# Loads in order of use, three weight groups, and a first feed-forward pass shared by two halves

## The chip, the cores and the metric

One core of a Trainium2 chip. The metric is the device time of one execution in microseconds; medians are over all runs of a kernel in one job, ratios over its fast runs alone. "The profile" is the trace of one execution; its clock starts at the span's start. Its engines: PE is TensorE (matmuls; PEld its weight loads), DVE VectorE, ACT ScalarE, POOL GpSimd, SP SyncE, which here only issues transfers.

## The reference, cut to what matters

Windowed attention with a few global keys, then a gated feed-forward block on its output. B = 4 batches, H = 8 heads, S = 768 positions, D = 64; the feed-forward goes 512 to 1536 to 512.

```python
scores = q @ k.T / sqrt(D) + bias          # per head
scores = where(is_global | is_local, scores, -1e9)   # 8 global keys, window of 96
a = softmax(scores)
x = (a @ v) as [B*S, H*D]                  # 3072 x 512
out = (maximum(x @ w_gate, 0) * (x @ w_val)) @ w_out
```

The kernel cuts the work into eight "halves" (a batch has two, of 384 positions). Each half needs its attention, then its feed-forward.

## The kernel before: the parts that the change touches

The loads, the one POOL queue that issues v and the weights, and the casts of q and k from fp32 to bf16 (for half 0: q on DVE, k on POOL):

```python
load_qk(0, 0, 2)                 # SP queue, heads 0 and 1 of half 0
...
nc.vector.memset(vbuf[0]...)     # ones, the whole buffer
load_qk(0, 2, 4)
load_v_globals(0); spread_v_globals(0)
load_v(0, 0) ... load_v(0, 3)    # POOL queue, casts fp32 to bf16
load_qk(0, 4, 8)
load_w(wgA, ...); load_w(wvA, ...)       # first 512 columns
load_half(1)                             # q, k and v of half 1
load_w(wgB, ...); load_w(wvB, ...)       # the other 1024 columns
load_w(wo_sb, ...)
...
eng = nc.vector if s == 0 and i == 0 else nc.gpsimd     # in piece_cast
```

The order of work: half 0's attention alone; then stages, in each of which one half's feed-forward pieces are woven with the next half's attention pieces. The schedule is fixed by hand, so each engine runs its instructions in this order:

```python
for i, (_, f) in enumerate(attention_pieces(0)):
    f()
    ...                          # masks of the later heads between pieces
nc.vector.memset(vbuf[1]...)     # fill of the second v buffer, here
...
for c in range(NHALF):
    if c + 2 < NHALF:
        load_half(c + 2)         # q and k on SP, three or five v loads on POOL
    a_items = attention_pieces(c + 1) if c + 1 < NHALF else []
    f_items = ffn_pieces(c)      # 24 gate/value pieces (4 matmuls each), 6 output pieces (6 each)
    ...                          # spread a_items over 0.9 of f_items
```

The softmax here doesn't subtract the row's maximum and nothing guards it: scores larger than these inputs give would overflow.

## Time and profile before

| | |
|---|---|
| median of 3 runs | 307.01 us (305.67 to 307.62) |
| profiled span | 302.9 us |
| PE busy | 247.9 us |
| PE idle up to 53 us | 37 us |
| one later stage | 31.7 us, about 2 us of it idle |

A row of the timeline reads: start, duration, engine, line, operation, tile written and tiles read, shape, count, and in brackets how long the engine had idled before and what ended that. L249 or L245 is the transpose of a head pair's q and k, the first step of its attention; "xT" is its last step. Between them lie kT (k transposed and put in its place), es (the exponentials of the scores, multiplied by the masks) and AV (es times v). I use three markers throughout: the *second transpose* of half 0, the end of the *last xT* of a half, and the *first transpose of half 3*.

### The profile page before, as it was taken

The numbers are of one execution on the slowest core, as the hardware profiler recorded it, in microseconds if no ns is written. First come the engines' busy times: TensorE is split into PE (matmuls) and PEld (weight loads), VectorE is DVE, ScalarE is ACT, GpSimd is POOL, SyncE is SP. The second block draws the span as 40 slices with busy tenths as digits, with TensorE's granted clock in tenths as the row PEclk, the third lists the DMA queues.
The fourth block names the chain that finished last, engine by engine and source line by source line (L and its number), as shares of the span: only waits on it lengthen the run. The fifth ranks groups of instructions, "written<-read, shape, count | busy, mean of one in ns | idle before, by whom it ended". The sixth has DMA issues, their size and how long they took to land.

```text
span 302.9 us, 4741 instructions
## 1 busy us (share of the span) xinstructions
PE 247.9 (82%) x1665; PEld 148.0 (49%) x1680; DVE 169.1 (56%) x477; ACT 168.3 (56%) x361; POOL 60.9 (20%) x105
## 2 busy tenths in 40 slices
PE   0025351998899889989898989988998899899995
PEld 0014230665466545655565546654664466545652
DVE  7624554567358644765466637773567457653420
ACT  1109640375737664767565765666575738664321
POOL 4940006913103400340226000400031000000000
PEclk9999999999999999999999999999999999999999
DMA  3999999905192614432760518001700110001002
GB/s 105 156 235 251 230 223 193 94 2 37 69 209 69 39 37 146 145 25 46 110 203 6 43 63 257 0 2 71 233 13 0 69 37 1 0 37 71 2 0 104
DMA packets 51208, 27.50 MB, mean 91 GB/s; under 512 B 27952, under 2 KB 46896, under 8 KB 51184
## 3 DMA queue, kind: packets, MB, share of 16 engines
q0 software_dynamic: 30800, 7.91, 25.5%
q1 hardware_dynamic: 20384, 19.30, 21.3%
q8 instruction: 13, 0.21, 0.3%
q14 instruction: 11, 0.09, 0.1%
HBM read 28.38 MB, written 6.29 MB: 114 GB/s over the span
## 4 chain that ended last, share of the span: by engine, by line
PE 69%; DVE 12%; ACT 10%; POOL 3%; DMA 3%; issue 3%; ACTq 0%; POOLq 0%
PE ff_ps L372 20%; PE ff_ps L363 18%; PE ff_ps L353 17%; DVE xT L331 6%; PE av_ps L314 5%; PE qk_ps L286 5%; PE tp L245 3%; DMA vbuf<-in_v_dram 3%; ACT lnd L323 2%; ACT grelu L356 2%; ACT rcp L328 2%; POOL vbuf L135 2%; DVE ht L365 1%; DVE qp L251 1%; DVE vbuf L399 1%
## 5 line engine op out<-in xcount | busy, mean ns | idle before, releaser
L372 PE MATMUL ff_ps<-wo_sb,ht 128*128 128x512 bf16 x273 | 67.2, 379 | 0.8
L365 DVE TENSOR_TENSOR ht<-ff_ps,grelu 128x384 bf16<-128x384 f32 x96 | 53.1, 554 | 24.3 <-PE ff_ps L363 21.6
L331 DVE TENSOR_TENSOR xT<-av_ps,rcp 64x384 bf16<-64x384 f32 x64 | 35.5, 555 | 46.2 <-ACT rcp L328 33.5
L356 ACT ACTIVATE grelu<-ff_ps 128x384 bf16<-128x384 f32 x96 | 47.3, 493 | 24.3 <-DVE ht L365 13.8
L353 PE MATMUL ff_ps<-xT,wgB 128*128 128x384 bf16 x256 | 52.0, 325 | 4.8 <-DVE ht L365 4.8
L363 PE MATMUL ff_ps<-xT,wvB 128*128 128x384 bf16 x256 | 52.0, 325 | 3.5 <-ACT grelu L356 3.5
L289 ACT ACTIVATE es<-qk_ps 128x432 bf16<-128x432 f32 (+2 forms) x96 | 49.1, 538 | 4.0 <-PE qk_ps L286 3.2
L298 DVE TENSOR_TENSOR es<-es,m_all 128x432 bf16<-128x432 bf16 (+6 forms) x144 | 40.6, 314 | 18.1 <-ACT es L289 17.0
L372 PEld LDWEIGHTS <-ht 128*128 128x128 bf16 x288 | 27.2, 97 | 26.9
L286 PE MATMUL qk_ps<-qp,kT 128*128 128x432 bf16 (+6 forms) x144 | 33.6, 303 | 7.9 <-ACT es L289 7.9
L245 PE MATMUL tp<-ident,qk 128*128 128x128 bf16 x192 | 17.8, 233 | 26.0 <-DVE qk L234 12.8
L323 ACT ACTIVATE lnd<-av_ps 64x384 f32<-64x384 f32 x64 | 31.0, 485 | 12.8 <-PE av_ps L314 11.1
L314 PE MATMUL av_ps<-es,vbuf 128*128 128x216 bf16 (+5 forms) x288 | 28.9, 236 | 7.2 <-DVE xT L331 6.6
L234 POOL CAST qk<-qs 128x384 bf16<-128x384 f32 x28 | 14.3, 510 | 101.0 <-DMA qs<-in_q_dram 35.0
L353 PEld LDWEIGHTS <-wgB 128*128 128x128 bf16 x256 | 23.8, 97 | 19.5 <-issue 6.4
L314 PEld LDWEIGHTS <-vbuf 128*128 128x128 bf16 x288 | 23.9, 102 | 17.3 <-issue 8.2
L363 PEld LDWEIGHTS <-wvB 128*128 128x128 bf16 x256 | 23.7, 97 | 17.4 <-issue 4.7
L135 POOL DMA_DIRECT2D vbuf<-in_v_dram x28 | 24.8, 894 | 22.4 <-PE av_ps L314 22.4
L245 PEld LDWEIGHTS <-qk 128*128 128x128 bf16 x192 | 14.0, 104 | 31.0 <-DVE qk L234 12.8
L353 PE MATMUL ff_ps<-xT,wgA 128*128 128x384 bf16 x128 | 28.0, 343 | 1.3 <-DVE xT L331 1.3
L363 PE MATMUL ff_ps<-xT,wvA 128*128 128x384 bf16 x128 | 27.4, 339 | 0.0
L377 ACT COPY osb<-ff_ps 128x512 f32<-128x512 f32 x24 | 14.0, 585 | 23.2 <-PE ff_ps L372 22.9
(54 smaller groups left out, 153.5 us busy)
## 6 DMA issues: line engine op xcount, KB each, us to landing
out_dram<-osb SPq DMA_DIRECT2D x24, 256.0 KB, 2.0
qs<-in_q_dram SPq DMA_DIRECT2D x7, 768.0 KB, 5.5
ks<-in_k_dram SPq DMA_DIRECT2D x7, 768.0 KB, 7.9
vbuf<-in_v_dram POOLq DMA_DIRECT2D x24, 120.0 KB, 4.0
wo_sb<-in_moe_w_out_dram POOLq DMA_DIRECT2D x1, 1536.0 KB, 35.6
wgB<-in_moe_w_gate_dram POOLq DMA_DIRECT2D x1, 1024.0 KB, 25.4
wvB<-in_moe_w_val_dram POOLq DMA_DIRECT2D x1, 1024.0 KB, 29.5
wgA<-in_moe_w_gate_dram POOLq DMA_DIRECT2D x1, 512.0 KB, 11.3
```

Of the source, the lines that this page charges most:

```text
L245: nc.tensor.matmul(tp[:, i, n * 128 : (n + 1) * 128], lhsT=qk[:, i, n], rhs=ident, is_transpose=True, start=(i == 0 and n == 0), stop=(i = ...
L286: nc.tensor.matmul(ps[:, c : c + n_], lhsT=kt[:, j, :], rhs=qd[:, :, :, a : a + w], start=True, stop=True)
L289: nc.scalar.activation(es[:, 0:cols], ps[:, 0:cols], AF.Exp, bias=0.0, scale=scale)
L298: nc.vector.tensor_mul(e4, e4, mk)
L314: nc.tensor.matmul(av3[:, :, a : a + w], lhsT=vb[:, j, z0 : z0 + 128], rhs=es[:, c : c + NN * w].rearrange("k (n p) -> k n p", n=NN), star ...
L323: nc.scalar.activation(ln[o0 : o0 + 64], av[d0 : d0 + 64, 0:QH], AF.Ln, bias=0.0, scale=1.0)
L331: nc.vector.tensor_tensor(xT_of[s][r, p, :], av_of[s, p, e_][r, 0:QH], rc[r], op=ALU.mult)
L353: nc.tensor.matmul(psg[:, 0:QH], lhsT=wg_of(dc, fc), rhs=xT[:, dc, :], start=(dc == 0), stop=(dc == N_DC - 1))
L356: nc.scalar.activation(gr, psg[:, 0:QH], AF.Relu, bias=0.0, scale=1.0)
L363: nc.tensor.matmul(psv[:, 0:QH], lhsT=wv_of(dc, fc), rhs=xT[:, dc, :], start=(dc == 0), stop=(dc == N_DC - 1))
L365: nc.vector.tensor_tensor(ht[:, fc, :], psv[:, 0:QH], st["gr"], op=ALU.mult)
L372: nc.tensor.matmul(ps2, lhsT=ht[:, fc, n * 128 : (n + 1) * 128], rhs=wo_sb[:, fc, :], start=(fc == 0), stop=(fc == N_FC - 1))
```

## The change

The intent: order the loads by when they are used, cut gate and value weights into three column groups of 512, and let feed-forward work start while weights still come in. Halves 0 and 1 therefore share the first pass over the weights: groups 0 and 1 are used by half 0, then by half 1, and only then group 2 by both. The mask arithmetic partly moves from DVE to POOL, sixteen mask Exps become eight larger ones ahead of the attention, and most fills move to POOL.

```diff
-    load_qk(0, 0, 2)
...
+    for p in range(HP):
+        load_qk(0, 2 * p, 2 * p + 2)          # all of half 0 first
...
+    spread_v_globals(0)
+    load_w_group(0)
...
+    load_w_group(1)
+    load_v_half(1)
+    load_w_group(2)
     load_w(wo_sb, moe_w_out, 0, DM)
...
-            eng = nc.vector if s == 0 and i == 0 else nc.gpsimd
+            eng = nc.vector if s == 0 and (i == 0 or p == 0) else nc.gpsimd
...
+    def load_qk_after(s):                     # a 1-element DVE memset holds the load back
+        qs_of[s] = stage.tile(...); ks_of[s] = stage.tile(...)
+        for t in (qs_of[s], ks_of[s]):
+            nc.vector.memset(t[0:1, 0, 0:1], 0.0)
+        load_qk(s, 0, H)
...
+    for _, f in attention_pieces(0):
+        f()
+    load_qk_after(1)
+    f1_0, f2_0 = ffn_pieces(0)                # f1: 24 gate/value pieces, f2: 6 output pieces
+    G2 = 2 * GW                               # 8 pieces: one column group
+    weave(f1_0[0:G2], [])
+    a1 = attention_pieces(1)
+    weave(f1_0[G2 : 2 * G2], a1, 0.4, 1.4)    # what does not fit follows bare
+    rest_of_start()                           # fills for the second batch, on POOL
+    f1_1, f2_1 = ffn_pieces(1)
+    weave(f1_1[0 : 2 * G2], [])
+    load_qk_after(2)
+    load_v_half(2)
+    weave(f1_0[2 * G2 :], [])
+    load_qk_after(3)
+    load_v_half(3)
+    weave(f1_1[2 * G2 :] + f2_0 + f2_1, attention_pieces(2))
+
+    for c in range(2, NHALF):                 # stages as before
...
```

More of the change, by code (lines that the diff above doesn't have):

```diff
@@ L84 @@
     ident = const.tile([128, 128], BF16)
-    nc.vector.memset(ident, 0.0)
     vbuf = [const.tile([128, NT, (2 * H + 1) * D], BF16, name=f"vbuf{i}") for i in range(2)]
@@ L88, with w_of @@
     qp = [const.tile([128, 2, QH], BF16, name=f"qp{i}") for i in range(4)]
-    GA = 4
-    wgA = const.tile([128, N_DC, GA * 128], BF16)
-    wvA = const.tile([128, N_DC, GA * 128], BF16)
-    wgB = const.tile([128, N_DC, DFF - GA * 128], BF16)
-    wvB = const.tile([128, N_DC, DFF - GA * 128], BF16)
+    GW = 4
+    wg = [const.tile([128, N_DC, GW * 128], BF16, name=f"wg{i}") for i in range(N_FC // GW)]
+    wv = [const.tile([128, N_DC, GW * 128], BF16, name=f"wv{i}") for i in range(N_FC // GW)]
     wo_sb = const.tile([128, N_FC, DM], BF16)
     m_all = const.tile([128, H, 2, NN, WQ], BF16)
-    def wg_of(dc, fc):
-        t, f = (wgA, fc) if fc < GA else (wgB, fc - GA)
-        return t[:, dc, f * 128 : (f + 1) * 128]
-    def wv_of(dc, fc):
-        t, f = (wvA, fc) if fc < GA else (wvB, fc - GA)
-        return t[:, dc, f * 128 : (f + 1) * 128]
+    def w_of(t, dc, fc):
+        f = fc % GW
+        return t[fc // GW][:, dc, f * 128 : (f + 1) * 128]
     qs_of, ks_of = {}, {}
@@ L137, in load_v, with load_v_half @@
             in_=v[b, :, KT * j : KT * j + n, :].rearrange("h p d -> p h d"))
-    def load_half(s):
+    def load_v_half(s):
         b, half = divmod(s, 2)
-        load_qk(s, 0, H)
         if half == 0:
@@ L144, in load_half @@
             spread_v_globals(b)
-            for j in range(4):
-                load_v(b, j)
-        else:
-            for j in range(4, NT):
-                load_v(b, j)
+        for j in range(4) if half == 0 else range(4, NT):
+            load_v(b, j)
     def load_w(dst, src, f0, f1):
         nc.gpsimd.dma_start(out=dst, in_=src[:, f0:f1].rearrange("(c p) f -> p c f", p=128))
-    def ones_of(i, j0, j1):
-        t = vbuf[i][:, j0:j1, :].rearrange("p j (h z) -> p j h z", z=D)[:, :, 0 : 2 * H + 1 : 2, :]
-        nc.vector.memset(t, 1.0)
@@ L159, with load_w_group, fill @@
-    load_qk(0, 0, 2)
+    def load_w_group(i):
+        load_w(wg[i], moe_w_gate, i * GW * 128, (i + 1) * GW * 128)
+        load_w(wv[i], moe_w_val, i * GW * 128, (i + 1) * GW * 128)
+    def fill(eng, i, j):
+        eng.memset(vbuf[i][:, j, :].bitcast(mybir.dt.uint32), 0x3F803F80)
+    def load_qk_after(s):
+        qs_of[s] = stage.tile([128, H, NN * D], FP32, name="qs")
+        ks_of[s] = stage.tile([128, H, NN * D], FP32, name="ks")
+        for t in (qs_of[s], ks_of[s]):
+            nc.vector.memset(t[0:1, 0, 0:1], 0.0)
+        load_qk(s, 0, H)
@@ L160 @@
+    for p in range(HP):
+        load_qk(0, 2 * p, 2 * p + 2)
+    nc.vector.memset(ident, 0.0)
+    for j in range(3):
+        fill(nc.vector, 0, j)
+    dd = setupp.tile([128, 2, NN, WQ], FP32)
+    pos = setupp.tile([NG, NN, WQ], FP32)
+    relg = setupp.tile([NG, NN, WQ], FP32)
     rel = setupp.tile([128, NN, WQ], FP32)
-    nc.gpsimd.iota(rel, [[1, NN], [NN, WQ]], base=NG, channel_multiplier=-1,
+    sel = setupp.tile([128, NN, WQ], FP32)
+    steps = [[1, NN], [NN, WQ]]
+    nc.gpsimd.iota(pos, steps, base=0, channel_multiplier=0,
@@ L162 @@
                    allow_small_or_imprecise_dtypes=True)
+    nc.gpsimd.iota(relg, steps, base=0, channel_multiplier=-1,
+                   allow_small_or_imprecise_dtypes=True)
+    nc.gpsimd.iota(rel, steps, base=NG, channel_multiplier=-1,
+                   allow_small_or_imprecise_dtypes=True)
+    nc.gpsimd.affine_select(out=sel, in_=rel, compare_op=ALU.is_ge, fill=BIG, base=NG,
+                            pattern=steps, channel_multiplier=-1)
+    nc.gpsimd.affine_select(out=dd[:, 1], in_=sel, compare_op=ALU.is_ge, fill=BIG,
+                            base=NL - 1 - NG, pattern=[[-1, NN], [-NN, WQ]],
+                            channel_multiplier=1)
@@ new lines @@
+    ga = setupp.tile([NG, NN, WQ], FP32)
+    gb = setupp.tile([NG, NN, WQ], FP32)
+    gc_ = setupp.tile([NG, NN, WQ], FP32)
+    gd = setupp.tile([NG, NN, WQ], FP32)
+    nc.vector.tensor_scalar(gb, pos, float(KT + NL - 2), BIG, op0=ALU.is_gt, op1=ALU.mult)
+    nc.vector.tensor_scalar(ga, pos, float(NL - 1), BIG, op0=ALU.is_lt, op1=ALU.mult)
+    nc.vector.tensor_add(ga, ga, gb)
+    nc.vector.tensor_scalar(gd, relg, 0.0, BIG, op0=ALU.is_ge, op1=ALU.mult)
+    nc.vector.tensor_scalar(gc_, relg, float(NL - 1), 1.0, op0=ALU.is_le, op1=ALU.mult)
@@ L163 @@
+    nc.vector.tensor_mul(gd, gd, gc_)
+    nc.vector.tensor_add(gd, gd, gb)
+    nc.vector.tensor_copy(dd[:, 0], dd[:, 1])
+    nc.vector.tensor_scalar(dd[0:NG, 1], ga, float(NL), None, op0=ALU.add)
+    nc.vector.tensor_scalar(dd[0:NG, 0], gd, float(NL), None, op0=ALU.add)
     nc.gpsimd.affine_select(out=ident, in_=ident, compare_op=ALU.not_equal,
@@ L165 @@
                             channel_multiplier=1)
-    pos = setupp.tile([NG, NN, WQ], FP32)
-    nc.gpsimd.iota(pos, [[1, NN], [NN, WQ]], base=0, channel_multiplier=0,
-                   allow_small_or_imprecise_dtypes=True)
-    relg = setupp.tile([NG, NN, WQ], FP32)
-    nc.gpsimd.iota(relg, [[1, NN], [NN, WQ]], base=0, channel_multiplier=-1,
-                   allow_small_or_imprecise_dtypes=True)
-    nc.vector.memset(vbuf[0].rearrange("p j z -> p (j z)").bitcast(mybir.dt.uint32), 0x3F803F80)
@@ L173 @@
-    load_qk(0, 2, 4)
-    load_v_globals(0)
-    spread_v_globals(0)
-    load_v(0, 0)
-    load_v(0, 1)
-    load_v(0, 2)
-    load_v(0, 3)
-    load_qk(0, 4, 8)
-    load_w(wgA, moe_w_gate, 0, GA * 128)
-    load_w(wvA, moe_w_val, 0, GA * 128)
-    load_half(1)
-    load_w(wgB, moe_w_gate, GA * 128, DFF)
-    load_w(wvB, moe_w_val, GA * 128, DFF)
-    load_w(wo_sb, moe_w_out, 0, DM)
-    for t in qp:
-        nc.vector.memset(t[64:128, 0, :], 0.0)
-        nc.vector.memset(t[0:64, 1, :], 0.0)
@@ L191 @@
-    for p in range(HP):
-        nc.vector.memset(kT[0][p][:, 3, 32:128], 0.0)
-    dm = setupp.tile([128, NN, WQ], FP32)
-    df = setupp.tile([128, NN, WQ], FP32)
-    pa = setupp.tile([128, NN, WQ], FP32)
-    pb = setupp.tile([128, NN, WQ], FP32)
-    nc.vector.tensor_scalar(pa, rel, 0.0, BIG, op0=ALU.is_lt, op1=ALU.mult)
-    nc.vector.tensor_scalar(pb, rel, float(NL - 1), BIG, op0=ALU.is_gt, op1=ALU.mult)
-    nc.vector.tensor_add(dm, rel, pa)
-    nc.vector.tensor_add(dm, dm, pb)
-    nc.vector.tensor_copy(df, dm)
@@ L204 @@
-    ga = setupp.tile([NG, NN, WQ], FP32)
-    gb = setupp.tile([NG, NN, WQ], FP32)
-    gc_ = setupp.tile([NG, NN, WQ], FP32)
-    nc.vector.tensor_scalar(gb, pos, float(KT + NL - 2), BIG, op0=ALU.is_gt, op1=ALU.mult)
-    nc.vector.tensor_scalar(ga, pos, float(NL - 1), BIG, op0=ALU.is_lt, op1=ALU.mult)
-    nc.vector.tensor_add(ga, ga, gb)
-    nc.vector.tensor_scalar(dm[0:NG], ga, float(NL), None, op0=ALU.add)
-    nc.vector.tensor_scalar(ga, relg, 0.0, BIG, op0=ALU.is_ge, op1=ALU.mult)
-    nc.vector.tensor_scalar(gc_, relg, float(NL - 1), 1.0, op0=ALU.is_le, op1=ALU.mult)
@@ L214 @@
-    nc.vector.tensor_mul(ga, ga, gc_)
-    nc.vector.tensor_add(ga, ga, gb)
-    nc.vector.tensor_scalar(df[0:NG], ga, float(NL), None, op0=ALU.add)
-    def build_masks(h):
-        nc.scalar.activation(m_all[:, h, 0], df, AF.Exp, bias=0.0, scale=-slopes[h])
-        nc.scalar.activation(m_all[:, h, 1], dm, AF.Exp, bias=0.0, scale=-slopes[h])
+    for j in range(3, NT):
+        fill(nc.vector, 0, j)
+    for i, t in enumerate(qp):
+        nc.gpsimd.memset(t[64:128, 0, :].bitcast(mybir.dt.uint32), 0)
+        nc.gpsimd.memset(t[0:64, 1, :].bitcast(mybir.dt.uint32), 0)
+        if i == 0:
+            load_v_globals(0)
+            load_v(0, 0)
+            load_v(0, 1)
+        if i == 1:
+            load_v(0, 2)
+            load_v(0, 3)
@@ L223 @@
+    spread_v_globals(0)
+    load_w_group(0)
+    for p in range(HP):
+        nc.gpsimd.memset(kT[0][p][:, 3, 32:128].bitcast(mybir.dt.uint32), 0)
+        nc.gpsimd.memset(kT[0][p][:, 6, NG + 48 : 128].bitcast(mybir.dt.uint32), 0)
+    load_w_group(1)
+    load_v_half(1)
+    load_w_group(2)
+    load_w(wo_sb, moe_w_out, 0, DM)
+    for h in range(H):
+        nc.scalar.activation(m_all[:, h], dd, AF.Exp, bias=0.0, scale=-slopes[h])
     xT_of = {}
@@ L352, in gate @@
             for dc in range(N_DC):
-                nc.tensor.matmul(psg[:, 0:QH], lhsT=wg_of(dc, fc), rhs=xT[:, dc, :],
+                nc.tensor.matmul(psg[:, 0:QH], lhsT=w_of(wg, dc, fc), rhs=xT[:, dc, :],
                                  start=(dc == 0), stop=(dc == N_DC - 1))
@@ L362, in val @@
             for dc in range(N_DC):
-                nc.tensor.matmul(psv[:, 0:QH], lhsT=wv_of(dc, fc), rhs=xT[:, dc, :],
+                nc.tensor.matmul(psv[:, 0:QH], lhsT=w_of(wv, dc, fc), rhs=xT[:, dc, :],
                                  start=(dc == 0), stop=(dc == N_DC - 1))
@@ L378, in outp, with weave @@
                 nc.sync.dma_start(out=out_v[c, n], in_=osb)
-        items = []
+        f1 = []
         for fc in range(N_FC):
-            items.append((0.65, lambda fc=fc: gate(fc)))
-            items.append((0.65, lambda fc=fc: val(fc)))
+            f1.append((0.65, lambda fc=fc: gate(fc)))
+            f1.append((0.65, lambda fc=fc: val(fc)))
+        f2 = []
         for n in range(NN):
             for part in range(2):
-                items.append((1.3, lambda n=n, part=part: outp(n, part)))
-        return items
-    for h in range(2):
-        build_masks(h)
-    pieces = attention_pieces(0)
-    for i, (_, f) in enumerate(pieces):
-        f()
-        if i in (4, 8, 12):
-            h = {4: 2, 8: 4, 12: 6}[i]
-            build_masks(h)
-            build_masks(h + 1)
-    nc.vector.memset(vbuf[1].rearrange("p j z -> p (j z)").bitcast(mybir.dt.uint32), 0x3F803F80)
-    for p in range(HP):
-        nc.vector.memset(kT[0][p][:, 6, NG + 48 : 128], 0.0)
-        nc.vector.memset(kT[1][p][:, 3, 32:128], 0.0)
-        nc.vector.memset(kT[1][p][:, 6, NG + 48 : 128], 0.0)
-    for c in range(NHALF):
-        if c + 2 < NHALF:
-            load_half(c + 2)
-        a_items = attention_pieces(c + 1) if c + 1 < NHALF else []
-        f_items = ffn_pieces(c)
+                f2.append((1.3, lambda n=n, part=part: outp(n, part)))
+        return f1, f2
+    def weave(f_items, a_items, first=0.0, last=0.9):
         total = sum(t for t, _ in f_items)
@@ L414, with rest_of_start @@
             done += t
-            while ai < len(a_items) and (ai + 0.5) / len(a_items) * 0.9 * total <= done:
+            while (ai < len(a_items)
+                   and (first + (ai + 0.5) / len(a_items) * (last - first)) * total <= done):
                 a_items[ai][1]()
                 ai += 1
-        assert ai == len(a_items)
+        for _, f in a_items[ai:]:
+            f()
+    def rest_of_start():
+        for p in range(HP):
+            nc.gpsimd.memset(kT[1][p][:, 3, 32:128].bitcast(mybir.dt.uint32), 0)
+            nc.gpsimd.memset(kT[1][p][:, 6, NG + 48 : 128].bitcast(mybir.dt.uint32), 0)
+        for j in range(NT):
+            fill(nc.gpsimd, 1, j)
+    for _, f in attention_pieces(0):
+        f()
+    load_qk_after(1)
[14 more added lines that the diff above has]
+    for c in range(2, NHALF):
+        if c + 2 < NHALF:
+            load_qk(c + 2, 0, H)
+            load_v_half(c + 2)
+        f1, f2 = ffn_pieces(c)
+        weave(f1 + f2, attention_pieces(c + 1) if c + 1 < NHALF else [])
 _INS = ['q', 'k', 'v', 'n_global', 'n_local', 'moe_w_gate', 'moe_w_val', 'moe_w_out']
```

## The prediction

> **What bounds the kernel now.** I read the page first, then the table by stretches, then the chain in order of time, then the timeline of the first 70 us.
>
> ```profile
> span 302.9 us, 4741 instructions
> PE 247.9 (82%) x1665; PEld 148.0 (49%) x1680; DVE 169.1 (56%) x477; ACT 168.3 (56%) x361; POOL 60.9 (20%) x105
> ```
>
> PE is busy 248 of 303 us. The table by stretches (PE, PEld, DVE, ACT, POOL busy; granted clock; DMA share; GB/s) says where the other 55 us are.
>
> ```profile
> 10.00:19.00 9.00, 0.70 (x6) 0.44 (x7) 2.77 (x9) 1.20 (x4) 7.45 (x10) 1.00 1.37 205
> 19.00:30.00 11.00, 6.03 (x39) 4.08 (x38) 5.86 (x22) 7.62 (x22) 1.14 (x3) 1.00 1.32 245
> 30.00:41.40 11.40, 5.13 (x32) 3.38 (x30) 6.56 (x18) 7.57 (x17) 0.00 (x0) 1.00 1.14 230
> 41.40:53.00 11.60, 4.18 (x16) 1.59 (x13) 5.49 (x16) 2.05 (x5) 4.80 (x7) 1.00 1.33 202
> 53.00:85.00 32.00, 30.04 (x205) 17.98 (x208) 19.32 (x55) 19.04 (x41) 13.39 (x23) 1.00 0.54 51
> 85.00:117.00 32.00, 29.79 (x205) 17.85 (x206) 18.90 (x52) 20.21 (x44) 6.25 (x11) 1.00 0.46 89
> ```
>
> Up to 53 us PE works 16 us and idles 37; after that each 32 us stretch idles about 2. So only the first 53 us hold anything to win. From there a stage (one half's feed-forward woven with the next half's attention) lasts 31.7 us, the step between its first matmuls in the chain:
>
> ```profile
> 84.81 0.65 PE ff_ps L353 x4
> ...
> 116.52 0.65 PE ff_ps L353 x4
> ```
>
> The timeline splits the 37 us:
>
> ```profile
> 17.21 1.02 POOL L152 DMA_DIRECT2D wo_sb<-in_moe_w_out_dram  x1 [0.85 <-DMA vbuf<-in_v_dram]
> 18.23 0.96 POOL L234 CAST qk<-ks 128x384 bf16<-128x384 f32 x2
> 18.80 0.50 PE L245 MATMUL tp<-ident,qk 128*128 128x128 bf16 x3 [5.49 <-POOL qk L234]
> ...
> 20.88 0.80 PE L245 MATMUL tp<-ident,qk 128*128 128x128 bf16 x6 [1.58 <-DVE kT L264]
> ...
> 23.99 1.50 ACT L289 ACTIVATE es<-qk_ps 128x432 bf16<-128x432 f32 x3
> ...
> 42.67 1.14 DVE L331 TENSOR_TENSOR xT<-av_ps,rcp 64x384 bf16<-64x384 f32 x2 [1.85 <-ACT rcp L328]
> ...
> 44.67 3.23 DVE L399 MEMSET vbuf<- 128x3808 uint32 x1 [0.86 <-issue]
> ...
> 48.20 0.62 POOL L124 DMA_DIRECT2D vbuf<-in_v_dram  x1 [27.15 <-DVE vbuf L399]
> ...
> 52.99 0.94 PE L245 MATMUL tp<-ident,qk 128*128 128x128 bf16 x6 [6.09 <-POOL qk L234]
> ```
>
> To 18.8 us: the first k cast stands behind the weight issues on POOL, the last of which waits for a v load. From 18.8 to 43.8: attention of half 0 alone, 25.0 us of a chain through PE, ACT and DVE, PE half idle. From 46.9 to 53.0: POOL waits for the fill of the second v buffer, issues five v loads, and only then casts half 1, while PE waits 6.1 us. That last gap is an order of instructions, not missing weights.
>
> **What the Trainium skill says.** DMA: Bandwidth & Descriptors, "Issuing engines are not separate DMA queues": transfers started by different engines share the same 16 DMA engines. The trace agrees: between 24 and 30 us the two queues move nearly equal packet counts (571 and 571 in 24 to 26), each well below its rate alone. TensorE: Matmul & The Clock Gate, "What's actually happening": PE runs at half clock until it has been busy for about 3.4 us, and falls back after an idle window. The trace agrees: four 384-column matmuls take 1.28 us at 53.7 and 0.65 us from 56.2 on, 3.2 us after PE resumed. The same page, "Architectural detail" section on the array: ACT and DVE are strictly first-in first-out, POOL too per core. The trace agrees as far as it goes: the k cast waits behind an unrelated weight issue. I use all three.
>
> **The change part by part.**
>
> *Start.* All of half 0's q and k go first, the first pair is cast on DVE, so the first transpose can run near 9.5 us instead of 18.8. But k of the second head pair is still cast on POOL, after the issues of all weights. The compiled order shows the wo issue waiting for the semaphore lane of the group 0 value weights. So the second transpose needs that landing. Rates from the DMA view (queue: packets, MB, share) of 2 to 4, 8 to 10 and 48 to 50 us:
>
> ```profile
> q1 hardware_dynamic: 735, 0.53, 94.8%
> ...
> q0 software_dynamic: 1477, 0.18, 139.6%
> ...
> q0 software_dynamic: 406, 0.42, 124.3%
> ```
>
> q and k of half 0 are 8 x 256 = 2048 packets, 5.6 us at 735 per 2 us. v is 3904 packets, 5.3 us at 1477. Group 0 is 1024 packets of 1 KB, 5.0 us at 406. One after the other from 2.0 us: 17.9; plus 1 to 2 us to the semaphore: about 19. Then 1.0 us wo issue and 0.5 us cast: second transpose at 21.0, against 20.88. The early start is worth nothing there.
>
> *Attention of half 0.* From that transpose to the last xT it took 43.8 - 20.9 = 22.9 us. The mask Exps leave its ACT stream: es stood at 23.99 where kT had ended at 22.99 (1.0 us), and four masks at 28.4 to 29.6 held lnd back by about 1.0. The other four lay beside a DVE wait. So 20.9 us, end at 41.9.
>
> *First pass, half 0.* Eight pieces (group 0), then four of group 1 before the first transpose of half 1, since the weave places it at 0.49 of 5.2 us: 12 x 0.65 = 7.8 us, plus 1.6 for 3.2 us at half clock: 51.3. q and k of half 1 are now issued only after the last xT, at 42.0. Such a pair took 7.5 us in the steady part (issue 85.84, k cast 93.38), so cast by about 50.4: just in time. The 6.1 us gap is gone.
>
> *Attention of half 1.* Here is the price. In the kernel before it was woven through a whole stage and cost PE some 31.7 - 23.4 (96 x 0.163 + 36 x 0.217) - 2.1 idle = 6.2 us. Now only four pieces lie among its transposes and everything from the first AV on is bare. Half 0's own bare run is the measure: 25.0 us from first transpose to last xT, less 2.0 of masks, plus some 0.6 us DVE per head pair (five multiplies, 1.9 us, against four, 1.2), partly hidden, plus four feed-forward pieces whose ACT and DVE work (2 x 0.49 + 2 x 0.56) sits in the chain: 25.5 us. End at 76.8.
>
> *Half 1 groups 0 and 1, then group 2 of half 0.* 16 x 0.65 + 1.6 cold = 12.0, to 88.8; 8 x 0.65 = 5.2, to 94.0.
>
> *Rest woven with attention 2.* 8 x 0.65 + 72 x 0.217 = 20.8, attention 6.2, waits 1.5. q and k of half 2 are issued after half 1's 16 pieces, at 89.5, so cast at 97.6; the transpose comes after three pieces, at 96.0: 1.6 us stall. Sum 30.1, third stage starts at 124.1. In the kernel before it starts at 116.5. Three of four matmuls of the first gate run before the last xT at both bare ends, which takes off about 1 us.
>
> Sum: +6.6 to +7.6 us. From there both kernels run the same stages. 307 + 7 = 314.
>
> As a check by differences: half 0 ends 1.9 us earlier; the 6.1 us gap goes; half 1's attention costs 22.9 us (25.5 less the 2.6 of its four pieces) in place of 6.2, so +16.7; two stages' waits of 4.2 us become 1.5, so -2.7; the new stall is +1.6; half-clock time is about 3.2 us in both. Sum +7.6.
>
> **The rivals.**
> 1. *The intended gain comes:* loads ordered by use start attention at 10 us, everything ends 8 to 10 us earlier, about 298. For it: DMA is above 90% busy up to 50 us. Against: k of pair 2 still stands behind wo's issue on POOL, and 15.9 us of transfers come before that.
> 2. *The bare attention is shorter than I think* (20 us, since DVE and ACT are freer and masks are done): third stage at 118, about 309, no difference at 2%.
> 3. *The late q and k load becomes the bound:* wo is still moving at 42 us, as it was until 52.8 in the kernel before, the pair lands at 55 instead of 50, and half 1 begins 5 us later: about 319. Against: the software queue needs 4.7 MB at 0.21 MB per us, about 23 us from 12, so it should be empty by 38.
>
> **Range and chances.** Largest doubts: the bare attention (plus or minus 2.5 us), the second transpose (1.5), landings (2), together about 4 us. So 314 with 307 to 320. Slower by over 2% means above 313.1: 0.56. Within 2%: 0.38. Faster: below 300.9, only if the POOL argument is wrong: 0.06.
>
> **What would show it.** Second transpose between 19 and 23 us, preceded by a k cast on POOL directly after the wo issue. Last xT of half 0 near 42. No PE gap over 2 us between 42 and 51. Then 25 us, to about 77, with PE busy under half, and the matmuls after it at half clock for 3 us. Third stage starting near 124, stages from there 31.7 us apart. I am wrong if the second transpose runs before 15 us, or if half 1's attention takes under 20 us, or if PE loses time after the third stage has begun.

## The result

The changed kernel took 319.55 us (median of 4, 318.27 to 320.19), the kernel before 306.66 us in the same rounds. The ratio is 1.0415 (95% interval 1.0366 to 1.0465): slower. A ratio here is the mean time of one kernel's fast runs over the mean of the other's fast runs of the same rounds, so it is not quite the ratio of the medians. Two later controls of the same kernel gave 1.0346 and 1.0332.

The head of the page after:

```profile
span 316.5 us, 4810 instructions
PE 254.5 (80%) x1680; PEld 150.2 (47%) x1680; DVE 165.7 (52%) x461; ACT 168.2 (53%) x353; POOL 69.5 (22%) x139
```

The span grew by 13.6 us. PE is busy 6.6 us longer on the same work and idles 7 us more. (15 matmul records are missing from the trace of before, 1665 of 1680.) Half-clock matmuls, found below, are part of the 6.6 us; how large a part was not summed. The table by stretches, cut at the new phases (columns: PE, PEld, DVE, ACT, POOL busy; granted clock; DMA share; GB/s):

```profile
41.50:50.40 8.90, 8.85 (x45) 4.90 (x45) 2.86 (x7) 2.86 (x6) 0.66 (x2) 1.00 0.61 179
50.40:74.80 24.40, 13.03 (x105) 8.78 (x103) 14.96 (x47) 14.03 (x31) 13.69 (x30) 0.80 0.53 34
74.80:92.00 17.20, 17.20 (x94) 9.77 (x94) 6.15 (x13) 5.89 (x12) 0.00 (x0) 0.88 0.19 53
92.00:128.00 36.00, 28.60 (x177) 15.53 (x176) 16.57 (x45) 17.60 (x37) 14.03 (x24) 0.95 0.71 125
128.00:160.00 32.00, 29.58 (x214) 17.85 (x212) 19.76 (x57) 20.56 (x44) 7.81 (x13) 1.00 0.38 86
```

From 41.5 to 50.4 half 0's first pieces keep PE full: the old 6.1 us gap is gone. (The column of the granted clock does not show every slow spell: it reads 1.00 here, though four 384-column matmuls take 1.28 us at 43.1 and 0.65 us at 45.2. So "half clock" in what follows goes by the durations of matmuls.) From 50.4 to 74.8 half 1's attention runs nearly bare, and PE works 13 of 24.4 us. From 74.8 to 92 it is full again, first at half clock. From 92 to 128 the last weave idles 7.4 us where an ordinary 32 us stage idles about 2.4. The timeline after, at the points that answer to those shown of before:

```profile
19.40 1.02 POOL L141 DMA_DIRECT2D wo_sb<-in_moe_w_out_dram  x1 [1.66 <-DMA wv<-in_moe_w_val_dram]
20.41 1.41 POOL L238 CAST qk<-ks 128x384 bf16<-128x384 f32 x3
20.99 0.50 PE L249 MATMUL tp<-ident,qk 128*128 128x128 bf16 x3 [9.43 <-POOL qk L238]
...
40.36 1.14 DVE L335 TENSOR_TENSOR xT<-av_ps,rcp 64x384 bf16<-64x384 f32 x2 [1.85 <-ACT rcp L332]
...
50.44 0.71 PE L249 MATMUL tp<-ident,qk 128*128 128x128 bf16 x6
...
73.61 1.14 DVE L335 TENSOR_TENSOR xT<-av_ps,rcp 64x384 bf16<-64x384 f32 x2 [1.92 <-ACT rcp L332]
...
96.29 0.34 PE L249 MATMUL tp<-ident,qk 128*128 128x128 bf16 x3 [2.08 <-POOL qk L238]
...
123.31 0.66 PE L318 MATMUL av_ps<-es,vbuf 128*128 128x216 bf16 x4 [2.06 <-DVE xT L335]
123.82 2.72 PE L376 MATMUL ff_ps<-wo_sb,ht 128*128 128x512 bf16 x6
...
130.71 0.50 PE L249 MATMUL tp<-ident,qk 128*128 128x128 bf16 x6
```

and the last of these points, half 3's first transpose, in the kernel before:

```profile
118.30 0.50 PE L245 MATMUL tp<-ident,qk 128*128 128x128 bf16 x6
```

POOL waits 1.7 us for a value weight load, issues wo, and only then casts k of the second head pair; PE has waited 9.4 us for that, most of it while POOL issued the other loads. Half 0's last xT ends at 41.5 (43.8 before), half 1's first transpose stands at 50.4 (53.0 before), so up to here the change is ahead by 2.5 us. Half 3's first transpose stands at 130.71, against 118.30 before: 12.4 us behind. So the change loses 15 us between those two points, and at the second of them all but 1.2 us of the longer span is there.

### The profile page after: what moved, and what is told of

It is laid out like the page before. It is cut to its first block, busy times and chain, and to the rows that moved or that the text cites. A ratio compares the mean times of both kernels' runs of the same rounds, so it can differ in the third digit from the quotient of the medians.

```text
span 316.5 us, 4810 instructions
## 1 busy us (share of the span) xinstructions
PE 254.5 (80%) x1680; PEld 150.2 (47%) x1680; DVE 165.7 (52%) x461; ACT 168.2 (53%) x353; POOL 69.5 (22%) x139
## 4 chain that ended last, share of the span: by engine, by line
PE 63%; ACT 13%; DVE 12%; DMA 5%; POOL 3%; issue 3%; SPq 0%; ACTq 0%; POOLq 0%; DVEq 0%
PE ff_ps L376 18%; PE ff_ps L367 17%; PE ff_ps L357 16%; DVE xT L335 6%; PE av_ps L318 5%; PE qk_ps L290 4%; ACT lnd L327 4%; ACT rcp L332 3%; DMA wv<-in_moe_w_val_dram 3%; DMA ks<-in_k_dram 2%; PE tp L249 2%; ACT es L293 2%; ACT grelu L360 2%; DVE qp L255 2%; DVE qp L254 1%
## 5 line engine op out<-in xcount | busy, mean ns | idle before, releaser
L357 PE MATMUL ff_ps<-xT,wg 128*128 128x384 bf16 x384 | 81.2, 334 | 6.7 <-DVE ht L369 3.4
L367 PE MATMUL ff_ps<-xT,wv 128*128 128x384 bf16 x384 | 80.2, 332 | 2.6 <-ACT grelu L360 2.6
L376 PE MATMUL ff_ps<-wo_sb,ht 128*128 128x512 bf16 x288 | 69.6, 384 | 0.0
L367 PEld LDWEIGHTS <-wv 128*128 128x128 bf16 x384 | 36.9, 99 | 31.9 <-issue 11.9
L357 PEld LDWEIGHTS <-wg 128*128 128x128 bf16 x384 | 37.1, 100 | 28.2 <-issue 7.3
L302 DVE TENSOR_TENSOR es<-es,m_all 128x432 bf16<-128x432 bf16 (+6 forms) x144 | 41.9, 325 | 16.0 <-ACT es L293 14.5
L318 PE MATMUL av_ps<-es,vbuf 128*128 128x216 bf16 (+5 forms) x288 | 30.3, 245 | 9.4 <-DVE xT L335 9.0
L318 PEld LDWEIGHTS <-vbuf 128*128 128x128 bf16 x288 | 24.9, 106 | 23.9 <-issue 15.8
L249 PEld LDWEIGHTS <-qk 128*128 128x128 bf16 x192 | 13.6, 102 | 28.8 <-POOL qk L238 13.7
L128 POOL DMA_DIRECT2D vbuf<-in_v_dram x28 | 24.3, 876 | 11.2 <-PE av_ps L318 11.2
L266 ACT COPY kT<-tp 128x360 bf16<-128x360 bf16 x16 | 7.3, 459 | 36.1 <-DVE qp L255 34.8
L290 PEld LDWEIGHTS <-kT 128*128 128x128 bf16 x144 | 14.5, 104 | 21.3 <-issue 12.0
```

What stands on the lines that cost most here:

```text
L249: nc.tensor.matmul(tp[:, i, n * 128 : (n + 1) * 128], lhsT=qk[:, i, n], rhs=ident, is_transpose=True, start=(i == 0 and n == 0), stop=(i = ...
L290: nc.tensor.matmul(ps[:, c : c + n_], lhsT=kt[:, j, :], rhs=qd[:, :, :, a : a + w], start=True, stop=True)
L302: nc.vector.tensor_mul(e4, e4, mk)
L318: nc.tensor.matmul(av3[:, :, a : a + w], lhsT=vb[:, j, z0 : z0 + 128], rhs=es[:, c : c + NN * w].rearrange("k (n p) -> k n p", n=NN), star ...
L357: nc.tensor.matmul(psg[:, 0:QH], lhsT=w_of(wg, dc, fc), rhs=xT[:, dc, :], start=(dc == 0), stop=(dc == N_DC - 1))
L367: nc.tensor.matmul(psv[:, 0:QH], lhsT=w_of(wv, dc, fc), rhs=xT[:, dc, :], start=(dc == 0), stop=(dc == N_DC - 1))
```

## The experiments

Twelve runs were made, of nine edited kernels, the unedited one twice and one edit a second time, all with correct results. They ask four things: what the bare attention costs, what the start is worth, what held up the last weave, and whether a better version exists.

### The price of the bare attention

**The new start with the old order of work** (woven).

```diff
-    for _, f in attention_pieces(0):
-        f()
-    load_qk_after(1)
-    ...                                   # the whole shared first pass
+    for i, (_, f) in enumerate(attention_pieces(0)):
+        f()
+        if i == 15:
+            load_qk_after(1)
-    for c in range(2, NHALF):
+    for c in range(NHALF):                # every half a stage; half 2's fills and v loads
+        ...                               # go in after half 1's casts
```

> The start of the changed kernel (loads, masks, casts, three weight groups) with the order of work of the kernel before: half 1's attention woven through the whole feed-forward of half 0, then stage after stage; q and k of half 1 let go in the middle of half 0's attention. Theory (the bare attention of half 1 is the price, and the start itself is a small gain): half 0's attention ends at about 41.5 as in the changed kernel, no 6 us gap, the third stage begins at 41.5 + 1.6 + 2 x 31.7 = about 106.5 instead of 128.1, so 319.6 - 21.6 = 298, 8 to 9 us under the kernel before. Rival (the new start itself is what costs): the time stays above 310.

Measured 297.25 us (295.47 to 297.47), ratio to before 0.9659. Half 0's last xT ended at 42.7 and half 3's first transpose stood 20.5 us ahead of the changed kernel:

```profile
110.19 0.50 PE L249 MATMUL tp<-ident,qk 128*128 128x128 bf16 x6
```

The rival, that the new start itself costs, falls. This edit also moves loads, so by itself it does not name the bare attention; the next one does.

**The kernel before, with only half 1's attention made bare** (before_bare).

```diff
+            if c == 0 and nth < 12:
+                continue                  # no attention piece among the first twelve
-            while ai < len(a_items) and (ai + 0.5) / len(a_items) * 0.9 * total <= done:
+            while ai < len(a_items) and (c == 0 or (ai + 0.5) / len(a_items) * 0.9 * total <= done):
```

> The kernel before with one edit: in the first stage no attention piece is issued until twelve feed-forward pieces are done, then all of half 1's attention follows bare, then the rest of the feed-forward. Loads and start are those of before. Theory (running half 1's attention bare is the price): the twelve pieces hide the 6.1 us gap, but the bare attention costs 25 us in place of about 6, third stage at 126 to 127 instead of 116.5, so about 307.5 + 10 = 317. Rival (the price was in the late loads and the half-finished first pass over the weights): 307 or less, since the gap is hidden.

Measured 315.72 us, ratio 1.0263: about 8 us over before, 1.3 under the expected 317. The table by stretches of this run:

```profile
54.00:80.00 26.00, 15.26 (x101) 10.43 (x99) 15.96 (x46) 14.11 (x30) 13.24 (x22) 0.61 0.60 42
```

and half 3's first transpose:

```profile
127.55 0.50 PE L245 MATMUL tp<-ident,qk 128*128 128x128 bf16 x6
```

With the old loads, PE again works little more than half of the time (15.3 of 26 us, and at a mean clock of 0.61). Half 1's attention ran from 54.33 to 79.31, 25.0 us, and half 3's first transpose came 9.3 us later than before. So the order of work alone, without any new load, makes most of the loss.

**The kernel before, with only the 6.1 us gap taken out** (before_fill_early).

```diff
     for h in range(2):
         build_masks(h)
+    nc.vector.memset(vbuf[1]..., 0x3F803F80)
     pieces = attention_pieces(0)
...
-    nc.vector.memset(vbuf[1]..., 0x3F803F80)
```

> The kernel before with one edit: the fill of the second v buffer stands before half 0's attention on DVE, where DVE waits for k anyway. Theory (the 6.1 us wait of PE before half 1's first transpose is an order of instructions, not missing data): POOL issues half 2's v loads by about 31 us and casts half 1 by about 36, the 6.1 us gap goes, 307.5 - 6.1 = 301.4. Rival (DMA is the limit of the first 50 us): another wait of the same length takes its place, on weights of the second group or on wo, and the time stays within 1.5 us.

Measured 300.04 us, ratio 0.9777 (0.9716 to 0.9837: clear of no change, though not of 2%), which is 6.9 us of 308.3. Half 1's first transpose now waits for nothing:

```profile
48.80 0.85 PE L245 MATMUL tp<-ident,qk 128*128 128x128 bf16 x6
```

Half 3's first transpose came at 113.15, 5.2 us earlier. The gap was an order of instructions: one moved line wins about what it cost, while the same weights arrive over the same engines.

### What the start is worth

**All k casts of half 0 on DVE** (k_on_dve).

```diff
-            eng = nc.vector if s == 0 and (i == 0 or p == 0) else nc.gpsimd
+            eng = nc.vector if s == 0 else nc.gpsimd
```

> The changed kernel with one edit: all four k casts of half 0 on DVE, none on POOL. Theory (the second transpose stands behind the weight issues on POOL): the second transpose moves from 21.0 us to about 11 us, right after the first one's copies; half 0's last xT from 41.5 to about 32; the later parts keep their lengths but half 1's q and k then load beside the weights, which may cost some of it back. So 319.6 - 9.4 = 310, or up to 314 if the load is late. Rival (the transfers of the start are the limit, v or weights would be missing anyway): second transpose early, but the first AV or the first gate waits, and the time stays within 1 us of 319.6.

Measured 312.38 us (310.28 to 313.35), ratio 1.0155. The second transpose moved from 20.99 to 11.21, half 0's last xT ended at 32.1. Some came back, as allowed for:

```profile
43.00 0.34 PE L249 MATMUL tp<-ident,qk 128*128 128x128 bf16 x3 [1.84 <-POOL qk L238]
45.20 0.34 PE L249 MATMUL tp<-ident,qk 128*128 128x128 bf16 x3 [1.86 <-POOL qk L238]
```

These two waits for half 1's q and k follow from the load being issued at half 0's end, now beside the weights. Half 3's first transpose came at 122.79, 7.9 us ahead. The changed kernel's early start was held by the k casts in POOL's queue: in this run PE waited for neither v nor weights up to 55 us.

**Both edits together** (woven_k_dve): the woven version with the line above.

> The woven version with all k casts of half 0 on DVE as well. Theory (the two gains are independent: no wait behind the weight issues at the start, no bare attention later): second transpose at 11 us instead of 22, half 0's last xT at about 32 instead of 42.7, all later stages shift by that: 297.3 - 10 = 287 to 288. Rival (with attention done 10 us earlier the weights are late): the first pass waits for the second or third column group or wo, and 3 us or more of the 10 are lost.

Measured 298.3 us (297.44 to 299.0), ratio 0.9694. No gain over the woven version: the theory missed, and so did the rival as it was put. It was not weights that were late:

```profile
44.58 0.51 POOL L238 CAST qk<-ks 128x384 bf16<-128x384 f32 x1 [8.63 <-DMA ks<-in_k_dram]
```

Half 1's k, issued at 23.0 us, was awaited until 44.6; PE stood 8.63 us. The DMA view of 40 to 42 us (queue: packets, MB, share of 16 engines) shows why:

```profile
q0 software_dynamic: 254, 0.26, 76.1%
q1 hardware_dynamic: 254, 0.20, 39.8%
```

Both queues moved 254 packets. A lone q and k load moves 735 packets in 2 us (the prediction shows it); beside the weights it gets one packet of 768 B for each packet of 1 KB. This is what the Trainium skill states in DMA: Bandwidth & Descriptors, section "Queues, rings and completion order": an engine takes turns between the queues that have work, packet by packet. The trace agrees: from 28 to 42 us the two counts are nearly equal in every 2 us (at worst 275 and 246). Whether the profile's packet is the page's, which holds several descriptors, is not shown. Nor is this the whole delay: the load was issued at 22.5 us and its first packets moved at about 26, while the other queue moved 2428 packets; what held it until then stays open.

**The load moved to where the engines are free** (woven_early).

```diff
     spread_v_globals(0)
+    load_qk(1, 0, H)
     load_w_group(0)
...
         if i == 15:
-            load_qk_after(1)
+            load_qk_after(2)
```

> The woven version with k casts on DVE, and half 1's q and k let go at the start, right after half 0's (half 2's take their place in the middle of half 0's attention). Theory (the 10 us that the early attention won were lost only because half 1's q and k shared the DMA engines with the weights packet by packet and landed at 44.6 us): they land by about 27, no wait of PE before half 1's first transposes, half 0's last xT at 32 to 33, and the time is 298.3 - 9 = 287 to 290. Rival (the start has no more to give; something else is late then): v, a column group or wo is waited for, and the time stays at 295 or above.

Measured 287.14 us (286.57 to 287.67), ratio 0.9348. The 8.6 us wait is gone, and half 3's first transpose comes at 99.85. This version beats both kernels.

### What held up the last weave

My sum had given the last weave 30.1 us; it took 36.2, from 91.93 to 128.10. Who waited for whom in 92 to 130 us of the changed kernel (us in total, times, longest):

```profile
PE qk_ps L290 <- ACT es L293: 3.0, 2, 1.9
PE tp L249 <- POOL qk L238: 2.1, 1, 2.1
PE av_ps L318 <- DVE xT L335: 2.1, 1, 2.1
PE ff_ps L357 <- DVE xT L335: 0.5, 1, 0.5
PE tp L249 <- DVE kT L268: 0.3, 1, 0.3
```

8.0 us of waits, of which the 0.5 us lie after the weave's end, and 1.3 us more in the six matmuls at 123.8 that took 2.72 us instead of 1.46.

**Half 2's q and k let go earlier** (early_qk2).

```diff
     rest_of_start()
+    load_qk_after(2)
     f1_1, f2_1 = ffn_pieces(1)
     weave(f1_1[0 : 2 * G2], [])
-    load_qk_after(2)
```

> The changed kernel with one edit: the load of half 2's q and k is let go right after the attention of half 1 instead of after half 1's sixteen feed-forward pieces. Theory (that load costs only the one wait before the first transpose of half 2): the 2.1 us wait goes, nothing else moves, 319.6 - 2.1 = 317.5. Rival (late loads explain most of the loss): 5 us or more come back.

Measured 315.85 us, ratio 1.0269. The wait for the cast is gone. The 1.9 us wait for es is gone as well in this profile: here POOL's casts of half 3 begin at 103.30, after the pair of mask multiplies (102.70 to 103.10) that the next experiment is about. The control ratios of the unedited kernel span 1.0332 to 1.0415, so the gain is 0.6 to 1.5%, or 2 to 4.5 us, around the expected 2.1; against the lower control the intervals overlap. That late load is a small part of the loss.

**Half 3's loads let go later, twice** (qk3_late, qk3_late_again), **and the unedited kernel as a control** (after_again, after_control). In the first profile one pair of DVE mask multiplies took 2.51 us at 103 us, while POOL ran six casts of half 3 back to back; an undisturbed pair takes 0.40. The Trainium skill names such a thing: GPSIMD Engine Reference, section "Specifications", says that POOL's SBUF interfaces are shared with DVE and that they contend where a DVE instruction has two SBUF inputs. These multiplies have two.

```diff
-    load_qk_after(3)
-    load_v_half(3)
-    weave(f1_1[2 * G2 :] + f2_0 + f2_1, attention_pieces(2))
+    late = f1_1[2 * G2 :] + f2_0 + f2_1
+    late.insert(16, (0.0, lambda: (load_qk_after(3), load_v_half(3))))
+    weave(late, attention_pieces(2))
```

> The changed kernel with one edit: half 3's q, k and v loads are let go after sixteen of the twenty pieces of the last weave instead of before it, so that POOL's six casts of half 3 no longer fall at 103 to 106 us, where one pair of mask multiplies on DVE took 2.51 us instead of 0.40. Theory (POOL's casts held DVE up): that pair takes about 0.4 us, the 1.9 us wait of PE for es at 107.7 shrinks below 0.5, and the time falls by 1.5 to 2 us to about 317.8, unless half 3's later load makes a new wait. Rival (the slow multiply is not due to POOL): it is as slow as before and the time is the same.

Measured 315.3 us, ratio 1.0257, and the pair was quick. But this job had no control on its chip:

> The changed kernel unedited, once more, as a control for the small effects: its ratio to the kernel before was 1.0415 in the first job, while the two small edits came out at 1.0269 and 1.0257 in another. Theory (those edits each won about 1.5%, more than the 0.6% that the plain wait explains): again 1.039 to 1.044. Rival (the first job's ratio was high by chance, half-clock spells falling differently): 1.030 to 1.035.

319.54 us, ratio 1.0346 (1.0289 to 1.0403): below the range that I had set for the theory, inside the rival's. The pair took 2.92 us. So both again on one chip:

> The changed kernel unedited, as the control of the next run on the same chip: 1.035 to 1.042 of the kernel before, and again one pair of mask multiplies of 2 to 3 us near 103 us.

> Half 3's loads let go late, beside a control on the same chip. Theory (POOL's casts of half 3 hold up DVE's multiply, and PE waits 1.9 us for it, part of the last weave's missing 5 us): 2 to 4 us under the control, and the slow pair is gone. Rival: less than 1 us apart.

The control gave 317.84 us, ratio 1.0332; the edit 318.22 us, ratio 1.0320. They are the same, and the forecast of 2 to 4 us was wrong. But the control's profile shows no collision that could have been removed. The pair in the first profile of the changed kernel, and in the control's:

```profile
102.98 2.51 DVE L302 TENSOR_TENSOR es<-es,m_all 128x288 bf16<-128x288 bf16 x2 [0.79 <-ACT es L293]
...
105.36 0.76 DVE L302 TENSOR_TENSOR es<-es,m_all 128x288 bf16<-128x288 bf16 x2 [0.79 <-ACT es L293]
```

The casts begin as close behind the pair in both (0.09 and 0.07 us). So the collision happens in some executions and not in others. Where it fell it went with more than its wait of 1.9 us: the last weave took 36.2 and 36.3 us in the two profiles with the slow pair (the first one and after_again) and 32.7 us in the control's, which has no half-clock spell at its end either. The times of the three profiled executions are closer (318.27, 319.35 and 317.22 us), among other things because the control came to half 1's attention 1.6 us later than the first. How often the collision falls is not on record, so what moving these loads is worth where it does stays open.

**The last weave spread over more work** (wide_weave): early_qk2, and

```diff
-    weave(f1_0[2 * G2 :], [])
     load_qk_after(3)
     load_v_half(3)
-    weave(f1_1[2 * G2 :] + f2_0 + f2_1, attention_pieces(2))
+    weave(f1_0[2 * G2 :] + f1_1[2 * G2 :] + f2_0 + f2_1, attention_pieces(2))
```

> The changed kernel with half 2's q and k let go early (as in the earlier run, 1.0269 of the kernel before) and with half 2's attention woven through eight more feed-forward pieces: 26.0 us of PE work instead of 20.8. Theory (the last weave lost 5 us to waits because its 28 attention pieces stand too close together between long out-projection pieces): the 2.06 us wait of the last AV for xT and the 1 us wait for es shrink to the 0.6 to 0.7 us of an ordinary stage, and the half-clock spell after them goes; 3 to 5 us under the earlier run, a ratio of 1.011 to 1.017. Rival (those waits belong to attention 2 wherever it stands): 1.024 to 1.030 again.

Measured 312.07 us (311.04 to 313.29), ratio 1.0206 (1.0152 to 1.0259). The waits of PE between 86 and 126 us, first of the earlier run:

```profile
PE av_ps L318 <- DVE xT L335: 2.1, 1, 2.1
PE qk_ps L290 <- ACT es L293: 1.1, 1, 1.1
```

and then of this one:

```profile
PE qk_ps L290 <- ACT es L293: 1.1, 1, 1.1
PE av_ps L318 <- DVE xT L335: 0.6, 2, 0.4
```

Left out are waits for kT, 0.3 and 0.5 us.

The wait of the last AV shrank from 2.1 to 0.6 us. It is 2.1 us in all five other profiles that I compare here (the changed kernel three times, early_qk2, and qk3_late, which moves half 3's loads alone), so the close packing is shown as its cause. The half-clock spell behind it is gone as well, but the control's profile of the unedited kernel has none either, so that is no evidence for packing. The 1.1 us wait for es stayed. The ratio fell by 0.6%, some 2 us, where the theory had asked for 3 to 5: packing is a part of the last weave's loss, not all of it. The two runs were in different jobs and their intervals overlap, so 0.6% is no more than a likely size.

## Why the prediction was right, and where its sum was off

The direction and the mechanism held, and 319.55 lies in the range, at its upper end. The size did not: about 7 us were forecast, 12.9 came in this job and, by the ratios of the two controls, 10.6 and 10.2. Step by step:

| step | predicted | profile after |
|---|---|---|
| second transpose of half 0 | 21.0 | 20.99 |
| half 0's last xT ends | 41.9 | 41.5 |
| half 1's first transpose | 51.3 | 50.4 |
| half 1's attention to its last xT | 25.5 us, to 76.8 | 24.3 us, to 74.8 |
| sixteen pieces, half clock at first | 12.0 us, to 88.8 | 12.0 us, to 86.7 |
| group 2 of half 0 | 5.2 us, to 94.0 | 5.2 us, to 91.9 |
| last weave | 30.1 us, to 124.1 | 36.2 us, to 128.1 |

- *The start wins nothing* was right: the k cast stood directly behind the wo issue. k_on_dve shows that the casts' place in POOL's queue held it. The landing behind the wait was right too: about 19 predicted, wo issued at 19.4.
- *The 6.1 us gap goes* was right, and before_fill_early shows that it needed no new load order.
- *The bare attention is the price* was right, and before_bare shows it without the rest of the change: 25.0 us there, 24.3 here. My 25.5 was 1.2 too long.
- *Rival 2* (20 us bare) fell: 24.3 and 25.0. *Rival 3* (late q and k at half 1) fell: no wait there, though only just, the k cast stood at 50.25. (The recorded sums add up to 0.9 us to the 7.5 us of such a load without saying so, 42.0 to 50.4 and 89.5 to 97.6; measured were 8.6 and 8.1 us.) *Rival 1* failed for the reason given against it.
- *The last weave* is the term that was mis-sized. I allowed 1.5 us of waits, taken from an ordinary stage, and a 1.6 us stall: 3.1 us. In the profile after there were 7.5 us of waits within it and about 1.7 us of half clock (1.3 in the six matmuls, the rest in the AV matmuls beside them), which together are the 6.1 us that it took too long. The stall itself was nearly right (2.08). The other waits were for es (3.0, of which 1.9 belong to a collision that comes and goes), for the last AV (2.1) and for kT (0.3). In the control's profile, with neither collision nor half clock, the weave took 32.7 us: 2.6 us of the miss are steady, the other 3.5 fell in the profile read here and in after_again. An ordinary stage spreads 28 attention pieces over 21 us of feed-forward work, this one over 18.7; wide_weave shows that as the cause of the AV's wait.
- *About 1 us off* for gate matmuls that run before the last xT: against the kernel before nothing is won at the first bare end, where they ran early as well (41.41 against 43.86). But the steps of the sum leave them out, and each bare end saved 0.5 us by them. That is why half 1's first transpose came 0.9 us early where the last xT came 0.4 early, and why 12.0 against 12.0 us is luck: half clock lasted 4.1 us there (74.8 to 78.9), not 3.2, which costs what they saved.
- *From there both kernels run the same stages* was nearly right: the distance is 12.4 us at half 3's first transpose and 12.7 at half 7's (258.50 against 245.77). The span's last 0.9 us lies in and after the end.

What stays open: why the collision falls in some executions and not in others, and how much of the spread of the changed kernel (315.75 to 320.19 in its fast runs) is the collision and how much the half-clock spells. Its profiled runs had mean clocks of 0.97 and 0.948 where the woven version had 1.00.

## What to carry to other kernels

Work that is limited by a chain through several engines should lie among work that is limited by one engine; taking it out costs the whole chain (24 to 25 us here, where woven it lengthened a stage by about 6), and that is far more than the new load order won (2.5 us). Before reordering loads, ask the trace whether data was missing at all: of the two waits that PE had at the start, one was a cast queued behind DMA issues and the other a fill placed too late, and moving single lines won what a new load order did not. A load let go beside a long stream of weights is slow: from q's issue to k's cast it took 12.4 us in k_on_dve and 22.0 us in woven_k_dve, against 7.5 us in a later stage. So let it go where the other queue is idle, or accept that and let it go early. And read more than one profile before explaining a small wait: three profiles of the same kernel differed by 3.6 us in one phase.

## What the Trainium skill lacked or had wrong

- DMA: Bandwidth & Descriptors says that queues take turns packet by packet, but not what this does to a latency: half 1's k, of 768 B packets, was awaited until 21.6 us after its issue beside 1 KB weight packets (254 packets of each in 2 us), where a pair of q and k in a later stage takes 7.5 us from issue to cast.
- GPSIMD Engine Reference names the contention of POOL and DVE for SBUF without a size. SBUF — State Buffer, section "SBUF: two separate sides", has a rule: whichever of the two starts first gets the shared ports for its whole instruction. Start order alone does not tell the cases here apart. The first multiply of the pair began 0.09, 0.06 and 0.07 us before the first of six casts of some 0.5 us; it took 2.11 and 2.52 us in two profiles and 0.36 us in the third. That this contention is the cause was tested only by moving the casts.
- No page that I read says why a DMA issue on POOL should wait for an older load that it shares no data with: in this kernel the wo issue idled 1.66 us until a value weight load landed, and the k cast stood behind it. That the two share a completion semaphore is my reading, which no run tests.
